# The first sixteen rows of the modulation matrix's five pieces on ScalarE's queue

## The chip, the cores and the metric

The kernel runs on one core of one Trainium2 chip. The core has TensorE (PE, with its weight loads shown apart as PEld), VectorE (DVE), ScalarE (ACT), GpSimd (POOL) and SyncE (SP, which here only issues transfers). The metric is the device time of one execution in microseconds, the median over several runs; lower is better. Before the change it is 325.9 us, median of three runs between 325.29 and 326.6 us.

## The reference, cut to what matters

The program is one transformer block with adaptive layer norm: a vector `c` is turned into six vectors of 640 numbers, which shift, scale and gate the two halves of the block.

```python
# x: 1 x 2048 x 640, c: 1 x 640, w_mod: 640 x 3840, all bf16
mod = (silu(c) @ w_mod).reshape(1, 6, 1, 640)
sa, ca, ga, sb, cb, gb = (mod[:, i] for i in range(6))
h = layernorm(x) * (1 + ca) + sa          # sa, ca: the first 1280 columns of w_mod
x = x + ga * attention(h)                 # 32 heads of 20, a window of 256 keys
h = layernorm(x) * (1 + cb) + sb
x = x + gb * ((sigmoid(h @ w_gate) * (h @ w_up)) @ w_down)
```

The change concerns only how the first 1280 columns of `w_mod` reach the core. They make `sa` and `ca`, without which no row of the first norm can be multiplied by `wq`, `wk` or `wv`.

## The kernel before, in words

The 2048 rows are worked on in eight chunks of 256 rows (two blocks of 128). A chunk goes through norm, transposition, the products with `wq`, `wk` and `wv`, windowed attention, the output product, the second norm and the gated feed-forward part. TensorE works almost without a pause from its first product to its last.

All instructions are first collected as operations with their reads and writes. A written-out list of numbers, `PLAN`, then sets the order in which operations go to the engines: an entry divided by five is the operation's number, the remainder its engine (0 PE, 1 ACT, 2 DVE, 3 POOL, 4 SP). Each engine takes its operations strictly in that order, and an operation waits by semaphores for what it reads. A transfer is one operation (`dma`, line 533); it is issued by SP, or by ACT when the code says so.

The start of the program runs like this.

- SP issues three transfers of `x`: 256 rows of the second chunk (320 KB), then the two 128-row blocks of the first chunk (160 KB each). Behind them come the five pieces of `w_mod` that this case is about, then `wq` and `wk` in halves, more rows of `x`, `wv` and the other columns of `w_mod`.
- ACT issues one small transfer, the vector `c` (1.2 KB, tile `c_row`), then loads its function table and computes the tanh for `silu(c)` (lines 606 to 609). DVE spreads the result over the tile `silubc`.
- A piece of `w_mod` holds 128 of its 640 rows, one to a partition, and 1280 columns: 128 rows of 2560 bytes, 320 KB. The five pieces land side by side in the space of `wd`, the later weight of the feed-forward part, and the profile calls them `wd`. In the code they are `wm_ap[0]`, and `load_bulk` at line 593 issues them, one transfer and one resource `Rm[0][kt]` for each `kt` from 0 to 4.
- DVE takes the statistics of the first rows of `x` as soon as they are there (lines 741 and 743, tile `st`), POOL computes the inverse root (lines 747 and 749), DVE normalises (line 762, `x<-x,st`), and TensorE transposes the result (`M<-ident,x`).
- Between the transpositions TensorE forms `silu(c) @ w_mod` in five steps of ten products (`fnA`, called at line 724, in the profile `S<-silubc,wd`), one step for each piece, and DVE copies the ten numbers per partition out (`mA`, line 726). Then DVE, ACT and POOL scale and shift the transposed rows (`hT<-hT,mA`, lines 822 and 823), and the product with `wq` begins.
- Products with a tile of zeros (`zeros`, line 621, in the profile `S<-E`) keep TensorE occupied before and between these steps. The first ten of them are followed by the transpositions.

Of the kernel before, what the change touches and what calls it, by code (L numbers as in the profile page):

```python
# [305 lines left out]
def c_pe(n):  # L306
# [4 lines left out]
    76, 139, 89, 63, 84, 202, 94, 3, 8, 243, 38, 175, 245, 72, 182, 186, 192, 197, 99, 53, 58, 13, 33, 18, 48, 104,  # L311
    109, 114, 357, 352, 124, 119, 129, 134, 747, 362, 378, 383, 337, 342, 392, 767, 347, 752, 762, 205, 210, 215,
    220, 225, 230, 1164, 368, 373, 772, 757, 387, 440, 235, 450, 250, 255, 260, 265, 405, 270, 395, 275, 778, 280,
    285, 290, 295, 456, 447, 412, 783, 792, 787, 795, 835, 805, 302, 401, 144, 482, 462, 472, 477, 433, 423, 466,
    600, 605, 801, 842, 815, 67, 417, 427, 585, 590, 811, 436, 822, 596, 611, 485, 490, 535, 540, 500, 615, 505,
    497, 550, 622, 512, 1172, 546, 1187, 1167, 555, 650, 561, 655, 565, 572, 1182, 661, 635, 515, 625, 640, 647,
    1192, 521, 1540, 1177, 1198, 1203, 23, 28, 525, 1208, 631, 715, 825, 532, 154, 1454, 149, 169, 720, 727, 665,
    685, 690, 697, 1546, 1217, 831, 1555, 700, 705, 730, 672, 575, 735, 712, 675, 1462, 1213, 1561, 1224, 682, 1457,
    1570, 581, 905, 890, 920, 910, 925, 895, 1553, 1568, 43, 1477, 917, 932, 1576, 1610, 1467, 164, 901, 742, 1583,
    875, 1472, 1482, 1228, 1616, 1623, 1243, 1488, 1493, 845, 880, 887, 860, 1498, 850, 865, 974, 871, 1625, 979,  # L320
    1631, 1246, 857, 969, 1585, 1045, 1072, 1597, 1592, 950, 955, 1052, 1602, 961, 1640, 935, 940, 947, 985, 1015,
    984, 1646, 990, 1020, 2650, 1055, 997, 1231, 1503, 1238, 1027, 1067, 1000, 2656, 1062, 1005, 1280, 159, 1285,
    1291, 1638, 1030, 2670, 1653, 1012, 1122, 1607, 1507, 1655, 1662, 1117, 1035, 1435, 1112, 2676, 1440, 1041,
    2690, 1667, 1325, 1340, 2663, 2668, 2696, 1672, 1345, 1352, 1250, 1255, 2559, 314, 1514, 334, 329, 1102, 1107,
    1677, 3114, 174, 1330, 1337, 1261, 2710, 2703, 1446, 1265, 1270, 1295, 1420, 1300, 1310, 1682, 1687, 2562, 2716,
    1307, 1276, 2730, 1089, 1425, 1690, 1695, 2736, 1720, 1315, 2567, 2572, 2750, 1374, 1076, 1321, 2756, 1379,
    1702, 1432, 2577, 2708, 2683, 2728, 2688, 2743, 2723, 2748, 1725, 1355, 1735, 1740, 1705, 1732, 2582, 1526,
    1747, 2587, 1405, 1767, 1772, 2770, 1710, 1717, 2768, 2763, 2593, 2598, 2613, 1384, 2603, 1360, 2776, 1531,
    1367, 1777, 1757, 1752, 1762, 1521, 1390, 1395, 1402, 1516, 1536, 1410, 2790, 3122, 1417, 1389, 2807, 3117,
    2370, 3127, 2796, 2802, 309, 2375, 2355, 1125, 2382, 2830, 1152, 2360, 2367, 2812, 1783, 2608, 2788, 2618, 2415,  # L330
    2624, 2783, 2420, 2430, 2435, 2525, 2836, 1132, 2479, 1788, 2828, 1792, 1797, 2848, 2843, 2426, 2442, 2484,
    2850, 2400, 2460, 2530, 2856, 2868, 2628, 2537, 2510, 2515, 2445, 2521, 2870, 2876, 2405, 1084, 1804, 2412,
    2642, 2632, 2888, 2638, 2465, 2385, 2471, 2646, 2495, 2390, 2450, 2397, 2890, 2457, 2500, 2910, 2970, 2975,
    2985, 2990, 2863, 2823, 2896, 2507, 2996, 3132, 3137, 2982, 3205, 2915, 2489, 2494, 3211, 1156, 2922, 2883,
    1135, 2925, 1147, 2908, 2903, 2930, 2540, 2545, 2937, 2817, 1844, 1142, 3142, 3225, 1834, 2551, 1821, 1806,
    1813, 3148, 3218, 1818, 2940, 3231, 3237, 3242, 3153, 3168, 3158, 4284, 3095, 2945, 1910, 3100, 1827, 1915,
    2955, 3106, 2951, 3247, 3860, 3866, 3163, 1920, 1925, 1935, 1839, 2960, 1930, 1940, 1945, 3252, 1950, 3858,
    3223, 3173, 1868, 3878, 2966, 1961, 1099, 3880, 1955, 1995, 3262, 3257, 1967, 4302, 1970, 2000, 2005, 1975,
    4307, 1872, 3039, 324, 1094, 319, 3179, 3886, 1852, 3034, 3000, 1980, 1985, 1990, 2021, 2010, 3265, 2015, 3005,
    3011, 2030, 3270, 2027, 3277, 2035, 2055, 3900, 2060, 2065, 2070, 3873, 3898, 3853, 4312, 1882, 1887, 1857,  # L340
    1849, 3906, 3015, 2040, 2075, 3020, 3080, 2045, 3085, 1892, 3893, 3913, 3918, 3026, 3091, 2050, 3920, 2081,
    3926, 3280, 3295, 3285, 3292, 2090, 2095, 2100, 2105, 2110, 2115, 2120, 3940, 3300, 2125, 2141, 3044, 2087,
    3933, 3938, 5484, 3946, 3307, 2130, 2135, 2147, 3327, 2150, 3192, 2175, 2155, 2160, 2165, 2180, 2170, 2201,
    3960, 3977, 3972, 3050, 2185, 4287, 3982, 3055, 2190, 2195, 3049, 2235, 2210, 2215, 3966, 3061, 3196, 2207,
    2220, 4000, 3310, 2240, 2245, 2250, 2255, 2225, 2230, 3315, 1863, 1898, 1903, 1878, 4292, 5492, 1907, 3987,
    4006, 2261, 3322, 4020, 3065, 3332, 2267, 4026, 2310, 4013, 4018, 3070, 2270, 2275, 3077, 3342, 3347, 5487,
    3337, 2330, 4040, 3201, 3181, 3953, 3998, 3958, 4297, 3352, 5507, 5502, 3358, 4038, 2280, 2290, 2335, 4046,
    3186, 2315, 4060, 2320, 5512, 3363, 3367, 3372, 2287, 2340, 3379, 2327, 4053, 4033, 4058, 3993, 4066, 4078,
    2347, 4110, 4170, 4115, 4121, 4073, 4365, 4371, 2295, 2300, 2307, 4185, 4190, 2354, 4175, 4197, 4375, 4318,
    3393, 4181, 3382, 4323, 4332, 4387, 4381, 4392, 5048, 4140, 4145, 4151, 3388, 5497, 4327, 4080, 4085, 4155,  # L350
    4160, 5000, 5028, 3401, 4095, 4100, 4092, 4125, 5006, 4167, 4107, 5023, 4250, 4255, 4261, 4130, 4235, 4265,
    4136, 5060, 4270, 4220, 5013, 4225, 4232, 3430, 4240, 3396, 5066, 4397, 3435, 3440, 4247, 5018, 4276, 5033,
    5043, 5053, 5078, 5088, 5090, 5073, 3405, 3410, 3415, 3420, 3425, 3445, 3450, 3465, 3470, 3490, 5619, 5096,
    5108, 3495, 5120, 3500, 3505, 4204, 5103, 5113, 4402, 4412, 4219, 3456, 3510, 3475, 5083, 3480, 5126, 5058,
    3485, 3462, 3525, 3530, 3535, 3550, 3516, 3522, 3540, 3555, 3560, 3565, 3570, 3545, 3576, 3582, 5118, 4339,
    4407, 4361, 5038, 4346, 5130, 5147, 3610, 3615, 3620, 3625, 3630, 3585, 4343, 3590, 5518, 5523, 3595, 3600,
    4353, 5532, 5136, 3605, 3636, 5160, 5166, 3645, 3650, 5142, 5527, 5188, 5198, 3655, 3660, 3665, 3696, 3670,
    3675, 3680, 5539, 3685, 3642, 5183, 3690, 5220, 4460, 3702, 5208, 5218, 5226, 5203, 5213, 5178, 3730, 3735,
    3705, 3710, 3715, 3720, 3725, 3756, 3740, 5250, 5256, 4415, 4420, 4427, 5561, 3745, 3750, 3762, 4358, 4430,
    4435, 4442, 4209, 4445, 4450, 5233, 4214, 5243, 4465, 4457, 4472, 4492, 4497, 5565, 5571, 4477, 4482, 4487,  # L360
    5325, 5330, 5337, 5385, 5390, 5396, 5310, 5238, 5248, 5193, 5268, 5278, 5263, 5273, 5315, 5173, 5152, 5157,
    5322, 5280, 5285, 5575, 5355, 4502, 4508, 4513, 5291, 5295, 5300, 5592, 5360, 5367, 5340, 5345, 5352, 5587,
    5597, 5307, 5581, 6205, 6211, 6228, 6233, 6248, 3785, 3765, 3790, 6238, 6253, 5370, 3825, 6263, 5375, 5381,
    6265, 4517, 6218, 3770, 6271, 3805, 6243, 6223, 3830, 3795, 6278, 6295, 6283, 6258, 5541, 6293, 4522, 6301,
    6313, 6323, 4529, 4536, 5602, 3835, 3775, 5612, 3782, 3810, 3815, 3802, 6325, 6331, 5607, 3822, 3842, 5420,
    5425, 5431, 5650, 5620, 5625, 5655, 5662, 5632, 5665, 6308, 5670, 6318, 6288, 6335, 4533, 5677, 4553, 4555,
    6352, 5635, 5640, 5647, 4546, 6347, 4541, 4580, 6341, 4585, 4590, 5556, 4595, 4600, 6413, 4560, 6365, 4565,
    4570, 4575, 4615, 4620, 4625, 4630, 5419, 5697, 6371, 5702, 5707, 5547, 5404, 4635, 4640, 6393, 4645, 6425,
    4606, 4650, 4655, 4660, 4675, 4666, 4700, 4705, 4710, 5682, 4680, 4685, 4715, 6431, 4690, 4695, 5687, 5692,
    5713, 5718, 6423, 6383, 6443, 6408, 4672, 3849, 4720, 4760, 6455, 6388, 6398, 5414, 5722, 4726, 4735, 4740,  # L370
    6461, 4745, 4750, 5727, 5734, 6357, 6378, 6403, 6418, 6362, 4755, 4612, 4786, 4765, 4770, 4775, 4780, 6685,
    6691, 4795, 4800, 6473, 4792, 4805, 4810, 4815, 4820, 4825, 4732, 4830, 4835, 4840, 4880, 4885, 4890, 6438,
# [66 lines left out]
MW = 64  # L439
# [887 lines left out]
```

## Time and profile before

| | |
|---|---|
| median of three runs | 325.9 us (325.29 to 326.6) |
| the profiled execution's own time | 324.32 us |
| its span, first to last instruction | 322.6 us |
| PE busy | 316.8 us, 98% of the span |
| DVE, ACT, POOL busy | 62%, 67%, 60% |
| the chain that ended last | PE 89%, POOL 4%, ACT 3%, DVE 2%, DMA 1% |
| first product with `wq` | starts at 12.05 us |

Times in the profile count from the first instruction of the profiled execution. Its span is 1.7 us shorter than its own time, and its own time is 1.6 us below the median of the runs; what the change does is worked out inside the span and added to the median. In a row of a timeline the first number is the start and the second the length; a bracket at the end tells how long the engine stood idle before it and what ended that. In the chain of waits each row is a piece of the path that ended last, again start and length.

### The profile page before, as it was taken

The page shows a single profiled execution, that of the slowest core. Times are in us where ns is not written, and L with a number is a line of the kernel's source. Part 1 is how long each engine was busy: PE and PEld are TensorE (multiplying, and loading weights), DVE is VectorE, ACT ScalarE, POOL GpSimd, SP SyncE. Part 2 cuts the span into 40 slices and gives each one's busy share as a digit, 9 for nine tenths or more (in the row PEclk, how much of TensorE's full clock was granted, in tenths as well). Part 3 has the DMA queues.
Part 4 walks back from the last instruction along what each step waited for, and adds up shares of the span by engine and source line. Part 5 has one row for each costly group of instructions (what it writes and reads, how often), then busy time and mean ns, then how long its engine had stood idle before and what let it go on. Part 6 is the DMA issues. An engine that isn't in the chain of part 4 may idle for free.

```text
span 322.6 us, 11139 instructions
## 1 busy us (share of the span) xinstructions
PE 316.8 (98%) x4766; PEld 230.9 (72%) x4766; DVE 199.9 (62%) x424; ACT 214.6 (67%) x220; POOL 193.9 (60%) x334
## 2 busy tenths in 40 slices
PE   6999999999999999999999999999999999999997
PEld 2666656577776677766787667876788777877885
DVE  6796999677585545685557454676438453485422
ACT  1489999997798787859785858684768557200320
POOL 4338679788788596969393839585672836601000
PEclk9999999999999999999999999999999999999999
DMA  7999799999912343308250211420400021012111
GB/s 231 374 332 199 198 258 206 184 273 317 210 40 41 103 92 48 62 3 130 55 114 4 35 35 48 102 43 2 122 6 4 2 43 43 2 41 43 41 43 42
DMA packets 64619, 33.61 MB, mean 104 GB/s; under 512 B 49082, under 2 KB 63034, under 8 KB 64570
## 3 DMA queue, kind: packets, MB, share of 16 engines
q1 hardware_dynamic: 63744, 31.92, 42.3%
q10 hardware_dynamic: 826, 0.98, 0.9%
q8 instruction: 37, 0.61, 0.8%
q14 instruction: 12, 0.10, 0.1%
HBM read 18.35 MB, written 2.62 MB: 65 GB/s over the span
## 4 chain that ended last, share of the span: by engine, by line
PE 89%; POOL 4%; ACT 3%; DVE 2%; DMA 1%; issue 1%; SPq 0%; ACTq 0%; DVEq 0%; POOLq 0%
PE M L634 74%; PE S L635 8%; PE M L635 7%; POOL E L947 3%; ACT E L981 2%; DMA x<-in_A_x_dram 1%; DVE x L762 1%; DVE st L741 1%; POOL st L749 1%; POOL st L747 0%; ACT QT L664 0%; DVE hT L823 0%; DVE st L743 0%; ACT hT L777 0%; SPq L533 0%
## 5 line engine op out<-in xcount | busy, mean ns | idle before, releaser
L947 POOL TENSOR_SCALAR_AFFINE_SELECT E<-E 128x256 bf16<-128x256 bf16 (+2 forms) x234 | 149.3, 667 | 52.2 <-ACT E L981 34.5
L981 ACT ACTIVATE E<-S 128x2048 bf16<-128x2048 f32 x80 | 150.2, 1878 | 42.3 <-PE S L635 41.6
L634 PE MATMUL M<-h2T,wu 128*128 128x256 bf16 x480 | 66.4, 273 | 0.0
L634 PE MATMUL M<-h2T,wg 128*128 128x256 bf16 x480 | 65.8, 273 | 0.0
L1225 DVE SCALAR_TENSOR_TENSOR hh<-sig,M 128x512 bf16<-128x512 f32 x48 | 32.4, 681 | 43.8 <-ACT sig L1223 31.6
L634 PE MATMUL M<-wd,hh 128*128 128x320 bf16 (+2 forms) x396 | 56.4, 295 | 0.0
L634 PEld LDWEIGHTS M<-h2T,wu 128*128 128x128 bf16 x480 | 45.7, 98 | 8.1 <-issue 1.6
L634 PEld LDWEIGHTS M<-h2T,wg 128*128 128x128 bf16 x480 | 45.5, 98 | 8.3 <-issue 1.5
L634 PEld LDWEIGHTS M<-wd,hh 128*128 128x128 bf16 x396 | 37.0, 98 | 14.9 <-issue 1.4
L1223 ACT ACTIVATE sig<-M 128x512 f32<-128x512 f32 x48 | 28.4, 596 | 26.1 <-PE M L634 25.0
L635 PE MATMUL S<-QT,KT 20*64 20x64 bf16 (+5 forms) x1600 | 33.3, 231 | 0.5
L1112 DVE STREAM_TRANSPOSE T<-M 128x512 f32<-128x512 f32 x32 | 21.7, 698 | 12.2 <-PE S L635 10.0
L741 DVE BATCH_NORM_STATS2 st<-x 128x6 f32<-128x320 bf16 x64 | 28.3, 477 | 1.1 <-DMA x<-in_A_x_dram 0.8
L635 PEld LDWEIGHTS S<-QT,KT 20*64 20x64 bf16 (+1 forms) x1600 | 15.2, 99 | 18.4 <-ACT E L981 9.8
L634 PE MATMUL M<-wk,hT 128*128 128x320 bf16 x160 | 28.2, 300 | 0.0
L634 PE MATMUL M<-wv,hT 128*128 128x320 bf16 x160 | 28.0, 300 | 0.0
L634 PE MATMUL M<-wo,oT 128*128 128x320 bf16 x160 | 26.5, 300 | 0.0
L634 PE MATMUL M<-wq,hT 128*128 128x320 bf16 x160 | 26.0, 300 | 0.2 <-DVE hT L823 0.2
L1244 DVE TENSOR_TENSOR x<-M,x 128x320 bf16<-128x320 f32 (+2 forms) x33 | 15.4, 478 | 15.1 <-PE M L634 14.5
L1179 DVE TENSOR_TENSOR x<-M,x 128x320 bf16<-128x320 f32 x32 | 15.3, 487 | 13.6 <-PE M L634 13.0
L747 POOL TENSOR_SCALAR st<-st 128x2 f32<-128x2 f32 (+1 forms) x17 | 4.0, 233 | 32.7 <-DVE st L743 31.7
L635 PEld LDWEIGHTS M<-E,V 128*32 128x32 bf16 x960 | 19.9, 97 | 4.5 <-issue 2.2
(81 smaller groups left out, 298.9 us busy)
## 6 DMA issues: line engine op xcount, KB each, us to landing
x<-in_A_x_dram SPq DMA_DIRECT2D x11, 320.0 KB, 3.6
wd<-in_w_mod_dram SPq DMA_DIRECT2D x6, 320.0 KB, 5.0
wd<-in_B_w_down_dram SPq DMA_DIRECT2D x4, 480.0 KB, 5.3
out_dram<-x SPq DMA_DIRECT2D x5, 320.0 KB, 2.6
wg<-in_B_w_gate_dram SPq DMA_DIRECT2D x2, 576.0 KB, 6.9
wu<-in_B_w_up_dram SPq DMA_DIRECT2D x2, 576.0 KB, 6.2
wu<-in_w_mod_dram SPq DMA_DIRECT2D x1, 960.0 KB, 10.5
wq<-in_A_wqkv_dram SPq DMA_DIRECT2D x2, 400.0 KB, 6.7
```

The lines of the kernel that those rows point to most:

```text
L634: return e.matmul(o, l, r, start=st, stop=sp, skip_group_check=True)
L635: return e.matmul(o, l, r, start=st, stop=sp, tile_position=tp, skip_group_check=True)
L741: A("dve", lambda e, g, bi=bi, j=j: e.bn_stats(v(bi * 12 + j * 6, 6), src[bi].ap[:, j * 320:(j + 1) * 320]), 0.48, reads=[src[bi].r()], wr ...
L747: A("pool", lambda e, g, lo=lo, w=w: e.tensor_scalar(v(28 + lo, w), var()[:, lo:lo + w], EPS, None, op0=ALU.add), 0.2, reads=[st.r(("m", b ...
L749: A("pool", lambda e, g, lo=lo, w=w: e.tensor_tensor(v(30 + lo, w), v(28 + lo, w), mhalf[:, 0:w], op=ALU.pow), 0.71, reads=[st.r(("v", lo) ...
L947: return lambda e, eng: e.affine_select(dst(), src(), pattern=pattern, compare_op=ALU.is_ge, fill=0.0, base=base, channel_multiplier=mul)
L981: A("act", lambda e, eng: e.activation(dst(), src(Sp.ap), ACT.Exp, scale=SM_SCALE), 1.876, reads=[Sp.r()], writes=[E.r()], prio=3, tag=f"e ...
L1112: A("dve", lambda e, g, h=h: e.transpose(T1.ap[:, 512 * h:512 * h + 512], X[h].ap), 0.694, reads=[X[h].r()], writes=[T1.r(h)], prio=3.5, t ...
L1179: A("dve", lambda e, g, ps=ps, bi=bi, half=half: e.tensor_tensor(x1[bi].ap[:, half * 320:half * 320 + 320], ps.ap[:, 0:320], x1[bi].ap[:, ...
L1223: A("act", lambda e, g, pg=pg, sg=sg: e.activation(sg.ap[:], pg.ap[:], ACT.Tanh, scale=0.5), c_act(512), reads=[pg.r()], writes=[sg.r()], ...
L1225: A("dve", lambda e, g, pu=pu, sg=sg, f0=f0: e.scalar_tensor_tensor(out=hh.ap[:, f0:f0 + 2, :], in0=sg.ap[:].rearrange("p (a b) -> p a b", ...
L1244: A("dve", lambda e, g, ps=ps, bi=bi, c0=c0, n=n: e.tensor_tensor(x1[bi].ap[:, c0:c0 + n], ps.ap[:, 0:n], x1[bi].ap[:, c0:c0 + n], op=ALU. ...
```

## The change

The five pieces on SP's queue lose their first sixteen rows each: they now carry 112 rows, partitions 16 to 127. A new transfer on ACT's queue brings the sixteen rows of all five pieces at once: sixteen partitions, five rows of 2560 bytes in each. It has a resource of its own, `R_top`, and every one of the five steps of `silu(c) @ w_mod` now reads it too.

```diff
-    load_bulk(wm_ap[0], wm_src[:, :, 0:1280], Rm[0], 1.26, 0.2, "wm0")
+    R_top = R("wmtop")
+    dma(lambda: wm_ap[0][0:16, 0:5, :], lambda: wm_src[0:16, 0:5, 0:1280], 0.30, writes=[R_top], prio=0.2, tag="wmt", eng="act")
+    for kt in range(NDT):
+        p0 = 16 if kt < 5 else 0
+        dma(lambda kt=kt, p0=p0: wm_ap[0][p0:, kt:kt + 1, :], lambda kt=kt, p0=p0: wm_src[p0:, kt:kt + 1, 0:1280], 1.26,
+            writes=[Rm[0][kt]], prio=0.2 + 0.01 * kt, tag="wm0")
...
-        oA.append(A("pe", fnA, MW / 2400.0 * 10, reads=[Rm[0][kt], R_silubc], writes=[psA.r()], prio=0, lat=0.2, tag="modA", extra=wprev))
+        oA.append(A("pe", fnA, MW / 2400.0 * 10, reads=[Rm[0][kt], R_top, R_silubc], writes=[psA.r()], prio=0, lat=0.2, tag="modA", extra=wprev))
...
 PLAN = [
-    76, 139, 89, 63, 84, 202, 94, 3, 8, 243, 38, 175, 245, 72, 182, 186, 192, 197, 99, 53, 58, 13, 33, 18, 48, 104,
+    76, 91, 144, 89, 63, 84, 207, 99, 3, 8, 248, 38, 180, 250, 72, 187, 191, 197, 202, 104, 53, 58, 13, 33, 18, 48,
```

`NDT` is 5, so `p0` is always 16. The new operation is number 18, so all later numbers in `PLAN` grow by five; entry 91 puts it on ACT, second in the list. Apart from it no instruction changes its place on any engine.

The start of ACT's queue before, where `c_row` is the vector `c`:

```order
L291 UNCONDITIONAL_BRANCH [waits barrier_Pool_Activation_PE_DVE_SP_release]
L533 DMA c_row<-in_c_dram 5x128
L606 ACT_TABLE_LOAD
L606 ACTIVATE cth<-c_col 128x5 [waits sem_dve]
L664 ACTIVATE hT<-M 128x128 [waits sem_pe]
```

The same place in the changed kernel, whose lines from here on stand five lower in the file:

```order
L291 UNCONDITIONAL_BRANCH [waits barrier_Pool_Activation_PE_DVE_SP_release]
L533 DMA c_row<-in_c_dram 5x128
L533 DMA wd<-in_w_mod_dram 16x5x1280
L611 ACT_TABLE_LOAD
L611 ACTIVATE cth<-c_col 128x5 [waits sem_dve]
L669 ACTIVATE hT<-M 128x128 [waits sem_pe]
```

The new transfer stands behind `c` and ahead of the load of ScalarE's function table, so the table and the tanh that `silu(c)` needs are issued one transfer later.

The start of SP's queue before, with the three transfers of `x` and the five pieces:

```order
L291 UNCONDITIONAL_BRANCH [waits barrier_Pool_Activation_PE_DVE_SP_release]
L533 DMA x<-in_A_x_dram 128x2x640
L533 DMA x<-in_A_x_dram 128x640 x2
L533 DMA wd<-in_w_mod_dram 128x1280 x5
L533 DMA wq<-in_A_wqkv_dram 128x5x320 x2
L533 DMA wk<-in_A_wqkv_dram 128x5x320 x2
```

And in the changed kernel:

```order
L291 UNCONDITIONAL_BRANCH [waits barrier_Pool_Activation_PE_DVE_SP_release]
L533 DMA x<-in_A_x_dram 128x2x640
L533 DMA x<-in_A_x_dram 128x640 x2
L533 DMA wd<-in_w_mod_dram 112x1280 x5
L533 DMA wq<-in_A_wqkv_dram 128x5x320 x2
L533 DMA wk<-in_A_wqkv_dram 128x5x320 x2
```

Only the size of the five pieces differs; their number and their place behind `x` do not.

218 rows, old and new, of the table PLAN are left out of this document.

## The prediction

> **What bounds the kernel now.** I read the profile's page first, then the chain of waits over the first 16 us, because the change touches nothing later. The page:
>
> ```profile
> span 322.6 us, 11139 instructions
> PE 316.8 (98%) x4766; PEld 230.9 (72%) x4766; DVE 199.9 (62%) x424; ACT 214.6 (67%) x220; POOL 193.9 (60%) x334
> PE 89%; POOL 4%; ACT 3%; DVE 2%; DMA 1%; issue 1%; SPq 0%; ACTq 0%; DVEq 0%; POOLq 0%
> ```
>
> TensorE is busy all through, and only 1% of the chain that ended last is a transfer. That one is at the start (the chain of waits, start and length of each piece):
>
> ```profile
> 1.30 3.08 DMA x<-in_A_x_dram
> ...
> 4.41 1.28 DVE st L741 x3
> ...
> 6.20 0.59 POOL st L749
> 6.82 0.45 DVE x L762
> ...
> 8.84 0.41 DVE x L762
> ...
> 9.64 0.72 POOL st L749
> 10.39 0.81 DVE x L762 x2
> 11.19 0.09 DVE mA L726
> ...
> 11.38 0.55 DVE hT L823 x2
> ...
> 12.05 4.00 PE M L634 x31
> ```
>
> The path begins with the second transfer of x, in at 1.30 + 3.08 = 4.38 us, and runs without slack through VectorE and GpSimd to the first product with wq at 12.05. No piece of w_mod (wd in the profile) is on it. They are not waited for elsewhere either. The pieces' transfers, as a group, and the weight loads of the first and the fifth step that use them:
>
> ```profile
> L533 SPq DMA_DIRECT2D wd<-in_w_mod_dram x5: 432/432/432, 2.3 to 4.2; - x5
> ...
> DMA to landing us min/median/max: 4.5/5.2/5.9
> ```
>
> ```profile
> 7.77 0.39 PEld L634 LDWEIGHTS S<-silubc,wd 128*128 128x128 bf16 x10
> ...
> 10.38 0.55 PEld L634 LDWEIGHTS S<-silubc,wd 128*128 128x128 bf16 x10
> ```
>
> Issue plus landing gives 2.3 + 4.5 = 6.8 us for the first piece and 4.2 + 5.9 = 10.1 for the fifth, steps of 0.82 us. They are used at 7.77 and 10.38, so 1.0 and 0.3 us lie in between, and neither row has a bracket for a wait. TensorE comes late to them for its own reasons: it waits for x, as the transpositions ahead show.
>
> ```profile
> 2.72 4.44 PE L621 MATMUL S<-E 128*128 128x512 bf16 x10
> 7.32 0.40 PE L634 MATMUL M<-ident,x 128*128 128x128 bf16 x4 [0.16 <-DVE x L762]
> ...
> 8.12 0.59 PE L621 MATMUL S<-E 128*128 128x512 bf16 x2
> ...
> 10.60 0.45 PE L634 MATMUL S<-silubc,wd 128*128 128x64 bf16 x10
> 11.32 0.50 PE L634 MATMUL M<-ident,x 128*128 128x128 bf16 x6
> ```
>
> Even the end of the fifth step, 10.60 + 0.45 = 11.05, comes when VectorE is still at the x of the chain (10.39 + 0.81 = 11.20); the copy of mA behind it would gain nothing from an earlier step.
>
> **What the change gives.** Each piece on SP's queue shrinks from 320 to 280 KB, an eighth, so with 0.82 us a piece the fifth could land up to 5 x 0.82 / 8 = 0.5 us sooner. Nobody waits for it: the gain is **0**. SP still issues five transfers of 0.432 us; SP is not waited for. The bytes in all are the same, so wq and what follows it on the queue move neither way, except by what the queue loses or gains on the way.
>
> **What the change costs on ACT.** One more issue ahead of the function table (timeline, with SP's first issues above it):
>
> ```profile
> 0.79 1.43 SPq L533 DMA_DIRECT2D x<-in_A_x_dram  x3
> ...
> 0.79 0.57 ACTq L533 DMA_DIRECT2D c_row<-in_c_dram  x1
> 1.40 1.28 ACT L606 ACT_TABLE_LOAD   x1 [1.40 <-PEq L1312]
> 2.69 0.21 ACT L606 ACTIVATE cth<-c_col 128x5 f32<-128x5 bf16 x1
> ```
>
> ```profile
> 3.13 0.49 DVE L609 COPY silubc<-siluc 128x320 bf16<-128x320 bf16 x1
> 4.41 1.28 DVE L741 BATCH_NORM_STATS2 st<-x 128x6 f32<-128x320 bf16 x3 [0.78 <-DMA x<-in_A_x_dram]
> 5.60 0.19 DVE L743 BATCH_NORM_AGGREGATE st<-st 128x2 f32<-128x12 f32 x1
> 5.90 0.89 DVE L741 BATCH_NORM_STATS2 st<-x 128x6 f32<-128x320 bf16 x2
> ```
>
> An issue is 0.43 (SP) to 0.57 us (this row). Table, tanh and the copy to silubc come about 0.5 us later, the copy ends at 3.62 + 0.5 = 4.1, and VectorE then still waits for x until 4.38. The wait of 0.78 us covers it. Without that cover, or with an issue longer than 0.78 us, VectorE's statistics would start later by the excess. I take **0**.
>
> **What the change costs x.** This is the term that counts. The new transfer is issued at about 1.40 on ACT and can move from about 2.4 us: the first transfer of x is issued at 0.79 and the rows of the rates below show the engines half idle up to 2.5. Before, w_mod's first bytes stood behind all of x on one queue. Now 16 x 5 x 2560 bytes = 200 KB of it are on a second queue while x is under way, on the same DMA engines. The rates, over five stretches (length, busy time of each engine, clock, DMA share, GB/s):
>
> ```profile
> 1.90:2.50 0.60, 0.18 (x2) 0.12 (x3) 0.04 (x1) 0.60 (x1) 0.60 (x5) 1.00 0.62 53
> 2.50:4.00 1.50, 1.50 (x4) 0.56 (x5) 0.78 (x3) 0.39 (x2) 0.97 (x11) 1.00 0.96 351
> 4.00:5.20 1.20, 1.20 (x4) 0.45 (x3) 0.80 (x2) 0.00 (x0) 0.00 (x0) 1.00 0.96 166
> 5.20:6.20 1.00, 1.00 (x4) 0.37 (x3) 0.89 (x4) 0.00 (x0) 0.23 (x2) 1.00 1.01 378
> 6.20:10.00 3.80, 3.57 (x48) 2.01 (x47) 3.74 (x12) 0.28 (x1) 1.98 (x5) 1.00 1.04 386
> ```
>
> From 2.5 us on the engines are full (share 0.96), so whatever the new transfer moves, x loses. The third transfer of x also shows what happens where x gives way to w_mod:
>
> ```profile
> L533 SPq DMA_DIRECT2D x<-in_A_x_dram x1: 424/424/424, 1.8 to 1.8; - x1
> ...
> DMA to landing us min/median/max: 4.1/4.1/4.1
> ```
>
> It lands at 1.8 + 4.1 = 5.9. From x at 4.38 to the first piece at 6.75 (6.8 above) 480 KB arrive in 2.37 us, where 0.82 us for each 320 KB would make 1.23: 1.1 us are lost, and the row 4.00:5.20 shows where, at 166 GB/s with busy engines. That is the stretch in which w_mod is read for the first time. Whether that reading is the cause the trace does not tell.
>
> The bounds of the delay to x's second transfer, with 204,800 bytes:
> - below: **0**, if the engines serve SP's queue first, or if the new rows fit into the idle 38% of 1.90:2.50 (its 53 GB/s and share of 0.62 make that little).
> - at full rate: 204,800 / 386 GB/s = **0.53 us**.
> - at the rate of the stretch with w_mod's first rows: 204,800 / 166 = **1.23 us**.
> - above: stall and slow rate one after the other, 1.1 + 1.23 = **2.3 us**.
>
> I take **1.2 us**: the new transfer is w_mod's first read, so that row is the nearest. A gain is all but excluded, since x's second transfer cannot land sooner by a transfer that joins it; the only give is the 0.11 us before the statistics of the third transfer (5.60 + 0.19 to 5.90), and only if that transfer came sooner.
>
> From 4.38 the delay goes through one to one: statistics at 5.6 instead of 4.41, wq at about 13.25. The third transfer would have to be in by 5.90 + 1.2 = 7.1, the fifth piece by 10.38 + 1.2 = 11.6; both have more room than before. So has wq, issued behind the pieces. Past 12.05 the chain has no transfer in it that matters (DMA 1% in all, 3.1 us of x here), so nothing takes the delay back.
>
> **Sum.** 0 (pieces) + 0 (ACT) + 1.2 (x) = +1.2 us. On the profiled execution 324.32 + 1.2 = 325.5, a span near 323.8; on the median **325.9 + 1.2 = 327.1 us**, 0.37% more, which is inside what a measurement of this kernel tells from no change (about 0.5%, 1.63 us).
>
> **The rivals.**
> *Bandwidth alone.* The new rows move at the full rate and x loses 0.53 us: 326.4. For it: 378 to 386 GB/s as soon as the slow stretch is over. Against it: that stretch.
> *Hidden.* x keeps its place, or the new rows slip in unseen: 325.9. This is also the case in which the change does nothing that it says, because the pieces were never late. For it: x is issued 0.6 us before. Against it: the full engines from 2.5.
> *Clearly slower: the sixteen rows hold the engines.* All of them go to the first 16 of 128 partitions, an eighth of the memory's rows, while a full piece goes to all. If stall (1.1) comes on top of the bytes at full (0.53) to slow rate (1.23), x is 1.6 to 2.3 us late, 2.0 in the middle: 327.9. It decides from a delay of 1.63 on, that is x's second transfer after 6.0 us. For it: the engines stay busy in the slow stretch, so a slow packet blocks those behind it. Against it: no row here shows a transfer into few partitions with many bytes.
> [...]
> *The clock.* The ten zero products are about 0.43 us apart (4.44 us for ten), the pair at 8.12 0.2 us apart (0.59 less 0.38 of one), so TensorE doubles its pace around 7 us. The idle time ahead of the transpositions grows from 0.16 to 1.4 us. If the slow pace came back or stayed, the chain's 4.00 us of products from 12.05 would cost up to as much again: 327.1 + 1 to 4, say 329. Against it: the pace is up before the pause, and the pause is short beside the 4.4 us that it took.
> *Faster* needs a wait for w_mod that the trace does not have, or a queue without the stall of 1.1 us; of the latter only 0.11 us can reach the path: 325.8.
>
> **How the numbers follow.** Forecast (327.1) 0.36, bandwidth alone 0.27, hidden 0.12, sixteen rows hold the engines 0.18, clock 0.05, faster 0.02. The range leaves out the clock, the top of the slower case and the lower half of the hidden one: **325.7 to 328.0 us**. Slower by over 0.5% (above 327.53) are the clock, nearly all of the slower case and about a tenth of the forecast's weight: 0.26. Faster by over 0.5% (below 324.27): 0.02. Within 0.5%: 0.72.
>
> **What would show it.** In the changed profile the first statistics on VectorE start near 5.6 instead of 4.41, still ended by a transfer of x, and every later row up to wq (13.25) is as much later; the silubc copy ends near 4.1; the steps with w_mod show no wait for a transfer. The ACT transfer lands before 5.6. Right by the wrong way would be a later start whose bracket names silubc or ACT. Wrong would be statistics at 4.4 (then hidden), at 4.9 (bandwidth alone) or past 6.0 (slower), products after 7 us at half the pace (clock), or a step that waits for w_mod or wq.

## The result, and the profile after

The change made the kernel slower: 329.22 us median of six runs (328.57 to 329.35) against 325.88 us (324.52 to 326.8, six runs), a ratio of 1.0105 with a 95% interval of 1.0084 to 1.0126. The forecast was 327.1, within 325.7 to 328.0.

The page of the changed kernel. All line numbers from 594 on are five higher than before.

```profile
span 327.5 us, 11141 instructions
PE 318.1 (97%) x4766; PEld 232.0 (71%) x4766; DVE 199.6 (61%) x424; ACT 214.6 (66%) x220; POOL 194.4 (59%) x334
PE 88%; POOL 3%; DMA 3%; ACT 3%; DVE 1%; issue 1%; SPq 0%; ACTq 0%; DVEq 0%; POOLq 0%
```

The share of transfers in the chain that ended last went from 1% to 3%. Its start, from the chain of waits over the first 20 us (start, length):

```profile
1.30 5.31 DMA x<-in_A_x_dram
...
6.64 1.28 DVE st L746 x3
...
9.05 0.46 DVE x L767
...
10.52 0.83 PE S L626 x2
11.35 0.53 PE S L639 x10
...
14.71 0.18 DVE mA L731
...
15.66 4.41 PE M L639 x34
```

The second transfer of x takes 5.31 us instead of 3.08, so the statistics start at 6.64 instead of 4.41: **2.23 us**. From there to the first product with wq it was 7.64 us before (4.41 to 12.05) and is 9.02 now (6.64 to 15.66): another **1.38 us**, and the chain now runs through TensorE's zero products (L626) and the steps with w_mod (`S L639`), which were not on it before. The timelines of TensorE and VectorE at this place:

```profile
3.22 4.19 PE L626 MATMUL S<-E 128*128 128x512 bf16 x10
9.56 0.40 PE L639 MATMUL M<-ident,x 128*128 128x128 bf16 x4 [2.14 <-DVE x L767]
...
10.35 1.00 PE L626 MATMUL S<-E 128*128 128x512 bf16 x2
11.14 0.74 PE L639 MATMUL S<-silubc,wd 128*128 128x64 bf16 x10
```

```profile
3.73 0.49 DVE L614 COPY silubc<-siluc 128x320 bf16<-128x320 bf16 x1
6.64 1.28 DVE L746 BATCH_NORM_STATS2 st<-x 128x6 f32<-128x320 bf16 x3 [2.42 <-DMA x<-in_A_x_dram]
```

TensorE stands idle for 2.14 us ahead of the transpositions. Soon behind that the pair of zero products takes 1.00 us instead of 0.59, and the second step's ten products with w_mod 0.74 instead of 0.46, which were these before:

```profile
8.55 0.46 PE L634 MATMUL S<-silubc,wd 128*128 128x64 bf16 x10
```

The granted clock, by stretches (length, busy time of each engine, clock, DMA share, GB/s):

```profile
3.58:7.00 3.42, 3.42 (x9) 1.21 (x8) 0.96 (x3) 0.00 (x0) 0.00 (x0) 1.00 1.10 203
7.00:10.40 3.40, 1.26 (x19) 0.73 (x18) 3.12 (x11) 0.14 (x1) 1.04 (x3) 1.00 1.05 300
10.40:13.80 3.40, 3.40 (x38) 2.31 (x34) 2.64 (x8) 0.53 (x2) 1.53 (x3) 0.50 1.11 326
13.80:17.00 3.20, 2.98 (x41) 1.98 (x39) 2.18 (x10) 2.00 (x5) 0.84 (x2) 1.00 1.12 368
```

For 3.4 us TensorE runs at half the clock, right behind a stretch in which it was busy for 1.26 us of 3.40. The column shows this fall, but not the slow pace at the start of the program: it reads 1.00 in 3.58:7.00 too, where the ten zero products take 0.42 us each, about twice the later time (the pair at 14.51 takes 0.60 us and a single one 0.38, so 0.22 from one to the next). Whether the pace has come up at all must be read from the products.

A third loss comes later, at a wait for a transposing transfer. The same products before, and now:

```profile
33.71 0.40 PE L635 MATMUL S<-QT,KT 20*128 20x256 bf16 x8
```

```profile
38.54 0.40 PE L640 MATMUL S<-QT,KT 20*128 20x256 bf16 x8 [1.15 <-DMA QT<-stg]
```

The products of TensorE are 3.61 us late up to there and 4.83 us from there, and the span ends 4.95 us later (322.56 to 327.51). That is more than the medians differ, 3.34 us: the first profile of the kernel before, 324.32 us, was one of its quick executions. The experiments had to explain three things: why x is late, whether the half clock is the price of the pause, and whether the wait for QT belongs to the change.

### The profile page after: what moved, and what is told of

Its sections match the earlier page's. It is cut to its first block, busy times and chain, and to the rows that moved or that the text cites. A ratio compares the mean times of both kernels' runs of the same rounds, so it can differ in the third digit from the quotient of the medians.

```text
span 327.5 us, 11141 instructions
## 1 busy us (share of the span) xinstructions
PE 318.1 (97%) x4766; PEld 232.0 (71%) x4766; DVE 199.6 (61%) x424; ACT 214.6 (66%) x220; POOL 194.4 (59%) x334
## 4 chain that ended last, share of the span: by engine, by line
PE 88%; POOL 3%; DMA 3%; ACT 3%; DVE 1%; issue 1%; SPq 0%; ACTq 0%; DVEq 0%; POOLq 0%
PE M L639 72%; PE S L640 8%; PE M L640 7%; POOL E L952 3%; ACT E L986 2%; DMA x<-in_A_x_dram 2%; DMA QT<-stg 1%; PE S L626 1%; PE S L639 1%; POOL st L754 0%; DVE st L746 0%; DVE x L767 0%; ACT QT L669 0%; DVE hT L828 0%; ACT hT L782 0%
## 5 line engine op out<-in xcount | busy, mean ns | idle before, releaser
L639 PE MATMUL M<-h2T,wu 128*128 128x256 bf16 x480 | 66.4, 273 | 0.0
L639 PE MATMUL M<-h2T,wg 128*128 128x256 bf16 x480 | 65.8, 273 | 0.0
L639 PE MATMUL M<-wd,hh 128*128 128x320 bf16 (+2 forms) x396 | 56.4, 295 | 0.0
L639 PEld LDWEIGHTS M<-h2T,wu 128*128 128x128 bf16 x480 | 45.7, 98 | 8.2 <-issue 1.6
L639 PEld LDWEIGHTS M<-h2T,wg 128*128 128x128 bf16 x480 | 45.6, 98 | 8.2 <-issue 1.5
L639 PEld LDWEIGHTS M<-wd,hh 128*128 128x128 bf16 x396 | 37.0, 98 | 14.9 <-issue 1.4
L639 PE MATMUL M<-wk,hT 128*128 128x320 bf16 x160 | 28.2, 300 | 0.0
L639 PE MATMUL M<-wv,hT 128*128 128x320 bf16 x160 | 28.0, 300 | 0.0
L639 PE MATMUL M<-wo,oT 128*128 128x320 bf16 x160 | 26.5, 300 | 0.0
L639 PE MATMUL M<-wq,hT 128*128 128x320 bf16 x160 | 26.0, 300 | 0.2 <-DVE hT L828 0.2
```

Source lines behind the costliest of these rows:

```text
L639: return e.matmul(o, l, r, start=st, stop=sp, skip_group_check=True)
```

## The experiments

Theories at the start: **narrow**, the sixteen partitions of the ACT transfer make it hold the transfer engines while x is on them; against it **share**, any 200 KB beside x would cost as much. For the second loss: **clock** against slower pieces of w_mod.

### The same bytes over all partitions

```diff
-    dma(lambda: wm_ap[0][0:16, 0:5, :], lambda: wm_src[0:16, 0:5, 0:1280], ..., eng="act")
+    dma(lambda: wm_ap[0][:, 0:1, 0:800], lambda: wm_src[:, 0:1, 0:800], ..., eng="act")
...
-        p0 = 16 if kt < 5 else 0
+        c0 = 800 if kt < 1 else 0     # the pieces on SP: all rows, columns c0 to 1279
```

> The ACT transfer carries as many bytes (204,800) at the same place, but over all 128 partitions: 800 columns of the first piece, whose other 480 columns stay on SP's queue; pieces two to five are whole again. Theory 'narrow': it is the 16 partitions that make the transfer hold the engines, so here x pays its bytes alone, 0.5 to 0.8 us: statistics at 4.9 to 5.2, wq at 12.6 to 12.9, time up to 0.8 us above before (326.4 to 326.7), pieces in steps of 0.82 us. Rival 'share': any 200 KB of w_mod on a second queue beside x cost x 2.2 us: statistics at 6.6, time near 329.

VectorE's timeline, and the pieces on SP's queue as a group:

```profile
4.57 1.28 DVE L746 BATCH_NORM_STATS2 st<-x 128x6 f32<-128x320 bf16 x3 [0.55 <-DMA x<-in_A_x_dram]
```

```profile
L533 SPq DMA_DIRECT2D wd<-in_w_mod_dram x5: 432/432/441, 2.3 to 4.2; - x5
...
DMA to landing us min/median/max: 3.5/4.2/5.1
```

x is 0.16 us late, less than even "narrow" expected (0.5 to 0.8), wq starts at 12.27 and the time is 325.6 us against 325.81, ratio 1.0000 (0.9985 to 1.0016). Even the fifth piece lands sooner than before, 4.2 + 5.1 = 9.3 instead of 10.1, and nothing that can be told comes of it. "Share" falls: the second queue and the bytes cost next to nothing here (0.16 us), the shape does (2.23 us).

### The ACT transfer later

```diff
+PLAN.remove(91)
+PLAN.insert(PLAN.index(191) + 1, 91)     # 191: the tanh
```

> The changed kernel with the ACT transfer issued behind the tanh (about 2.9 instead of 1.4 us), so that most of x is in before it moves. Both theories of the delay: statistics at 4.4 to 4.8. It tells what is left of the loss when x is spared: 'narrow' lets the transfer and the 112-row pieces slow each other, fifth piece at 11.5 to 12.5, the fifth step of silu(c) @ w_mod waits for it, wq at 12.5 to 13.5 and 0.5 to 1.4 us above before; 'share' has the fifth piece at about 10.0 and the time of before (325.9).

```profile
4.37 1.28 DVE L748 BATCH_NORM_STATS2 st<-x 128x6 f32<-128x320 bf16 x3 [0.74 <-DMA x<-in_A_x_dram]
...
7.69 0.89 DVE L748 BATCH_NORM_STATS2 st<-x 128x6 f32<-128x320 bf16 x2 [1.94 <-DMA x<-in_A_x_dram]
```

The second transfer of x is on time, but the third is caught: its statistics start at 7.69 instead of 5.90. wq starts at 14.81, later than both theories said: the expectation counted only the pieces, not the third transfer of x, and TensorE was at the slow pace (its pair of zero products takes 1.04 us behind a pause of 1.78). The time is 328.45 us, ratio 1.0114 (1.0083 to 1.0146): no better than the change.

### The sixteen rows on SP's queue, behind x

```diff
-    dma(lambda: wm_ap[0][0:16, 0:5, :], ..., eng="act")
+    dma(lambda: wm_ap[0][0:16, 0:5, :], ..., eng="sp")
+PLAN.remove(91)
+PLAN.insert(PLAN.index(99), 94)          # ahead of the five pieces
```

> The changed kernel with the sixteen-row transfer issued by SP, behind x and ahead of the five 112-row pieces, so that x has the engines for itself. Theory 'narrow': statistics at 4.4, the sixteen-row transfer takes about 2 us by itself and the 112-row pieces land in steps of 0.95 us, so the fifth is in at about 12 and the first product with wq starts at 13.3 to 14.3. Rival, only the meeting with x is slow: 0.5 us for the sixteen rows, steps of 0.72 us, fifth at about 9.9, wq at 12.05.

The six transfers of w_mod as a group, and what waited for them:

```profile
L535 SPq DMA_DIRECT2D wd<-in_w_mod_dram x6: 424/427/432, 2.3 to 4.6; - x6
...
  PEld S L641: 2.3, 5
  PE S L641: 0.7, 3
...
DMA to landing us min/median/max: 4.5/5.8/7.0
```

With x spared (statistics at 4.32), the loss moves to w_mod. The sixteen rows land at 2.3 + 4.5 = 6.8, when before a whole piece was in; the last 112-row piece at 4.6 + 7.0 = 11.6 instead of 10.1. That is (11.6 - 6.8) / 5 = 0.96 us for a piece of 280 KB, where 320 KB took 0.82. Now the steps wait for their pieces, and wq starts at 13.16, just ahead of the range expected (one execution, 326.53 us, beside 326.81 for the kernel before, so the time itself shows no loss). The sixteen rows cost 1.2 us here, not 2: the third transfer of x is in at 5.6, they are in at 6.8. But the 112-row pieces are slow in themselves too; "only the meeting with x" falls.

### Fewer bytes

```diff
-    dma(lambda: wm_ap[0][0:16, 0:5, :], ...
+    dma(lambda: wm_ap[0][0:16, 0:2, :], ...
-        p0 = 16 if kt < 5 else 0
+        p0 = 16 if kt < 2 else 0
```

> The ACT transfer carries the sixteen rows of the first two pieces only (80 KB), pieces three to five are whole again. Theory 'narrow' with a delay that grows with the bytes: two fifths of 2.24, statistics at about 5.3, wq at 12.9 to 13.3; the two 112-row pieces in steps of 0.95, the whole ones in steps of 0.82. Rival, a fixed price for the meeting: statistics at 6.4 to 6.7 as in the changed kernel.

Statistics at 5.23: 0.82 us late for 2/5 of the bytes, where 2/5 of 2.23 is 0.89. The delay goes with the bytes. wq starts at 14.27, a microsecond later than expected: from the statistics to wq it takes 9.04 us, as in the changed kernel, and TensorE is at the slow pace again (one execution, 327.66 us). This is not a fall of the clock like that of the changed kernel. There the first products behind the pause are still quick; here they are slow at once and the ten zero products ahead of the pause were slow too (4.47 us), while the clock column, which shows the fall there, stays at 1.00. So the pace had not come up yet:

```profile
8.15 0.61 PE L639 MATMUL M<-ident,x 128*128 128x128 bf16 x4 [0.95 <-DVE x L767]
```

### The same rows into unused space, near and far

The five pieces are whole again, and the ACT transfer copies 204,800 bytes of w_mod to space that nothing reads yet: this adds bytes and leaves no work out.

```diff
+    dma(lambda: Eall[0:16, 2:6, :].rearrange("p s c -> p (s c)")[:, 0:6400]...,     # near
+    dma(lambda: Eall[0:128:8, 2:6, :].rearrange("p s c -> p (s c)")[:, 0:6400]...,  # far
         lambda: wm_src[0:16, 0:5, 0:1280], ..., eng="act")
```

> The five pieces are whole (128 rows) on SP's queue as before; the ACT transfer of 200 KB still reads the same sixteen rows of each piece at the same place, but writes them to space that is not used yet, partitions 0 to 15. It is a copy that nothing reads, 200 KB more than before moves. Theory 'narrow' (sixteen neighbouring partitions take the bytes slowly): x as late as in the changed kernel, statistics at 6.2 to 6.8, but the whole pieces then follow in steps of 0.82 us. Rival, that the 112-row pieces make x late: statistics at 4.4 to 5.0.

> The same copy into unused space, to every eighth partition (0, 8, ... 120) instead of 0 to 15: same source, queue, bytes and number of rows. Theory 'narrow by place' (the neighbouring partitions share a way in): half as much delay or less, statistics at 4.6 to 5.4. Rival 'narrow by number' (sixteen partitions anywhere, or 12.8 KB into one partition, are slow): statistics at 6.2 to 6.8 as with partitions 0 to 15.

Near: statistics at 6.57, so the sixteen-row transfer alone makes x late, without any 112-row piece; the whole pieces follow in steps of 0.82 us (7.8 to 11.1), as expected. Far: statistics at 4.44, but the comparison is not clean. ScalarE needed 0.68 us to issue it instead of 0.34, so it moved later (from 3.2 to 3.6 us one packet of it moves, 41 with near), and it then caught the third transfer of x (statistics of that at 6.89 instead of 5.90). By these times, number or place stays open; the next section has a measure that decides it.

### Number or place

The same copy, to 32, 64 and 128 partitions; the bytes are always 204,800. If place counts, the two copies to 64 partitions differ; if the number alone does, they are alike.

```diff
+    dma(lambda: Eall[0:32, ...][:, 0:3200],  lambda: wm_src[0:32, 0, 0:3200], ..., eng="act")
+    dma(lambda: Eall[0:64, ...][:, 0:1600],  lambda: wm_src[0:64, 0, 0:1600], ..., eng="act")
+    dma(lambda: Eall[32:96, ...][:, 0:1600], lambda: wm_src[32:96, 0, 0:1600], ..., eng="act")
+    dma(lambda: Eall[0:128, ...][:, 0:800],  lambda: wm_src[0:128, 0, 0:800], ..., eng="act")
```

> The same copy to partitions 0 to 31, 6400 bytes in each. [...] Rival 'number': about twice the delay of 64 partitions, half of that of 16: statistics at 5.3 to 5.7 here, but 4.7 to 5.0 with 64.

> As spare_near (whole pieces on SP's queue, a copy of 204,800 bytes that nothing reads on ACT's), but to partitions 0 to 63 with 3200 bytes in each. [...] Rival 'number': the delay falls with the number of partitions (2.2 at 16, 0.2 at 128), 64 give 0.3 to 0.6: statistics at 4.7 to 5.0.

> The same copy to 64 partitions that lie elsewhere, 32 to 95. [...] Rival 'number': the same as with 0 to 63, within 0.15 us.

> The same copy to all 128 partitions, 1600 bytes in each: the measure for the other three. Both theories: x late by its bytes alone at most, 0.1 to 0.5 us, statistics at 4.5 to 4.9; the pieces of w_mod behind it 0.5 us later than before at most.

The stretch from 3.8 to 4.8 us, in which the copy and x share the engines (columns as above, the last is GB/s), with partitions 0 to 15:

```profile
3.80:4.80 1.00, 1.00 (x3) 0.30 (x2) 0.19 (x1) 0.00 (x0) 0.00 (x0) 1.00 1.03 113
```

With 0 to 31:

```profile
3.80:4.80 1.00, 1.00 (x3) 0.30 (x2) 0.18 (x1) 0.00 (x0) 0.00 (x0) 1.00 1.00 193
```

With 0 to 63:

```profile
3.80:4.80 1.00, 1.00 (x3) 0.30 (x2) 0.39 (x1) 0.00 (x0) 0.00 (x0) 1.00 1.01 243
```

With 32 to 95:

```profile
3.80:4.80 1.00, 1.00 (x4) 0.41 (x3) 0.97 (x4) 0.00 (x0) 0.00 (x0) 1.00 0.98 319
```

With all 128:

```profile
3.80:4.80 1.00, 1.00 (x3) 0.30 (x2) 0.47 (x2) 0.00 (x0) 0.00 (x0) 1.00 1.14 402
```

| partitions | statistics start | late by | third transfer of x in | time, one execution | issue on ACT |
|---|---|---|---|---|---|
| 0 to 15 | 6.57 | 2.16 | 7.0 | 327.99 | 0.34 |
| 0 to 31 | 5.73 | 1.32 | 6.1 | 327.02 | 0.34 |
| 0 to 63 | 4.95 | 0.54 | 6.1 | 326.29 | 0.53 |
| 32 to 95 | 4.38 | 0 | 5.7 | 324.29 | 0.60 |
| 128 | 4.63 | 0.22 | 5.4 | 325.66 | 0.38 |

In all five the transfer engines are busy all the time (shares of 0.98 to 1.14), and the rate climbs from 113 to 402 GB/s. (The kernel before moves 216 GB/s in this stretch, with no copy at all: it has the slow stretch of w_mod's first read there. So the rates rank the five copies, and do not say what a copy costs.) The delay of the statistics mixes two things, how slow the copy is and how much of x's second transfer it meets. The issues differ by up to 0.26 us, and from 3.2 to 3.6 us 20 packets of the copy move with 0 to 31, 5 with 0 to 63 and none with 32 to 95. That can be why 0 to 31 looks 0.8 us worse than 0 to 63 here, although the third transfer of x lands at 6.1 with both.

A measure without that is the time that the copy's own packets take on the 16 engines. The rows of ACT's queue, which carries nothing else of size, from 3 to 6 us (packets, MB, share of the 16 engines' time), with 0 to 15 and with every eighth partition:

```profile
q10 hardware_dynamic: 96, 0.20, 34.9%
```

```profile
q10 hardware_dynamic: 96, 0.20, 25.0%
```

With 0 to 63, and with 32 to 95:

```profile
q10 hardware_dynamic: 80, 0.20, 22.7%
```

```profile
q10 hardware_dynamic: 80, 0.20, 18.1%
```

Each pair has the same bytes, the same number of partitions and the same number of packets, and its two edits differ by place alone: place counts, and number alone falls. The share is 20.9% with 0 to 31, close to the 22.7% with 0 to 63, and 18.2% with all 128, close to the 18.1% with 32 to 95. The second of each pair also starts later, but an early start is not what raises the share: the 200 KB over all partitions of the first experiment start earlier than 0 to 63 (12 packets from 3.2 to 3.6 us) and have 18.2% too. Why 0 to 31 and 0 to 63 still differ a little is open; they also differ in what each partition takes (6400 and 3200 bytes).

### The clock: a shorter pause, and a longer one

The changed kernel with eight zero products more, and the kernel before with four fewer:

```diff
-HEAT = (5, 1, 1, 1, 1, 1, 1)
+HEAT = (13, 1, 1, 1, 1, 1, 1)     # in the changed kernel
+HEAT = (1, 1, 1, 1, 1, 1, 1)      # in the kernel before
```

> The changed kernel with 8 more zero products in the first block, so that TensorE is busy from 3.2 to about 9.0 us. Theory 'clock': the granted clock fell to half from 10.4 to 13.8 us because TensorE stood idle for 2.1 us behind the zero products; with the pause filled it stays up, x is as late as in the changed kernel (statistics at 6.64), and the first product with wq comes at about 14.3 instead of 15.66, 1.3 us or so off the time of the changed kernel: near 327.9. Rival: the 1.4 us between 9.56 and 15.66 come from something else (late pieces of w_mod, slower engines); then wq stays near 15.7 and the time near 329.2.

> The kernel before with 4 zero products fewer in the first block: TensorE is idle from about 5.3 to 7.3 us while x and w_mod are on time. Theory 'clock': statistics at 4.41 as before, clock at half until about 10.4, wq at 13.2 to 13.4 instead of 12.05, 1.2 us slower than before (327.1). Rival, the clock does not matter in this stretch: wq within 0.2 us of 12.05 and no difference in time.

TensorE in the changed kernel with more zero products:

```profile
2.73 5.63 PE L626 MATMUL S<-E 128*128 128x512 bf16 x18
9.32 0.40 PE L639 MATMUL M<-ident,x 128*128 128x128 bf16 x4 [0.96 <-DVE x L767]
...
10.12 0.60 PE L626 MATMUL S<-E 128*128 128x512 bf16 x2
```

And in the kernel before with fewer:

```profile
2.72 2.77 PE L621 MATMUL S<-E 128*128 128x512 bf16 x6
7.21 0.61 PE L634 MATMUL M<-ident,x 128*128 128x128 bf16 x4 [1.71 <-DVE x L762]
...
8.69 1.04 PE L621 MATMUL S<-E 128*128 128x512 bf16 x2
```

With the pause cut to 0.96 us the pair is back at 0.60 us, and statistics to wq take 7.65 us (6.40 to 14.05): the whole 1.38 us is gone with x still late. Its median is 328.03 us, 1.2 us below the changed kernel's from the earlier comparison, ratio to the kernel before 1.0091 (1.0066 to 1.0116). So the pause is what the 1.38 us hang on, and slower pieces are not needed for it. In the other, with x on time, the same stretch grows to 9.21 us (4.29 to 13.50), and the time is 326.82 against 325.81, ratio 1.0047 (1.0024 to 1.0070). But this is a neighbouring case, not the same one: its six zero products are slow (2.77 us) and so are the first products behind the pause (0.61), with 1.00 in the clock column throughout. There the pace came up late; it did not fall.

### The wait for QT in the kernel before

The kernel before, unchanged, twice more, and once with the transfer of wo that stands between the transposing transfers put ahead of them:

```diff
+PLAN.remove(164)
+PLAN.insert(PLAN.index(169) + 1, 164)    # wo ahead of the first transposing transfer
```

> The kernel before once more, to see an execution other than the one profiled at first (324.32). Theory 'chance': the wait of 1.15 us for a transposing transfer (QT<-stg) at 38.5 us of the changed kernel is not the change's doing; it is in most executions of the kernel before too, and an execution near 325.9 shows it, at 33.7 us, with everything up to there as in the first profile. Rival 'knock-on': the late start of the changed kernel causes it; then no execution of the kernel before shows it, and one near 325.9 loses its time elsewhere.

> As before_again: a further execution of the kernel before. By 'chance' an execution above 325.5 has a wait of about 1 us for QT<-stg near 33.7 us and one below 325 has none; by 'knock-on' neither has it.

> The kernel before with SP's first transfer of wo issued ahead of the transposing transfer of hT instead of behind it, at about 14.3 instead of 25.05 us, so that SP's issue of 1.26 us no longer stands between the transposes. Theory 'chance': QT<-stg is issued about a microsecond sooner, the wait goes, and the time settles near 324.4 instead of 325.9, 0.4% less. Rival: the wait comes from the transfers themselves or from more bytes ahead of hT; no difference, or up to 1.2 us slower.

The first took 324.95 us and has no such wait. The second took 326.75 us, and its waits between 30 and 40 us have the row

```profile
PE S L635 <- DMA QT<-stg: 1.4, 1, 1.4
```

Its wq starts at 13.01 instead of 12.05. TensorE's pace came up later (the single zero product ahead of the pair takes 0.63 us instead of 0.38), but the path goes elsewhere: four of the five steps wait for their piece of w_mod, and the chain of waits from 6 to 14 us begins with the last piece, in at 4.16 + 7.35 = 11.51 instead of 10.1.

```profile
7.69 0.63 PE L621 MATMUL S<-E 128*128 128x512 bf16 x1
...
8.58 0.60 PE L621 MATMUL S<-E 128*128 128x512 bf16 x2
```

```profile
4.16 7.35 DMA wd<-in_w_mod_dram
...
11.56 0.48 PE S L634 x10
```

So the kernel before has the wait for QT now and then, without the change, and "knock-on" in its strict form falls: the wait is no mark of the change. The runs above agree. It is absent with the copy to partitions 0 to 15, whose x is as late as in the changed kernel, and there with 128 partitions (1.07 us), whose x is not. A weaker form stays open: a wait of 0.4 to 1.4 us is there in 9 of the 12 profiled executions with an added transfer of w_mod, and in 1 of the 5 in which w_mod came as before. With wo ahead, ten runs had a median of 324.78 us (324.49 to 325.61) against 325.64 (324.17 to 326.15), but the ratio, 0.999, has an interval of 0.9972 to 1.0008: no difference that can be told.

## Why the prediction was wrong

Two steps failed. The term for the delay of x, 1.2 us, measured 2.23; and the clock, which cost 1.38 us more, was set beside that delay as a rival instead of behind it as its consequence.

- **Right, but only for the execution that was read: the gain of 0.** The pieces were not waited for there, and landing them 0.8 us sooner, with the bytes spread over all partitions, bought nothing that can be told. The slack of 0.3 us was thinner than one profile shows: in another execution of the kernel before one step waited 0.2 us for its piece, and in the third profile the last piece was on the path. That the gain is 0 on the median was in part luck.
- **Right: ACT's issue at no cost.** It took 0.34 us; the copy to silubc ends at 3.73 + 0.49 = 4.22, where 4.1 was expected, and VectorE's bracket names x.
- **Mis-sized: the delay to x.** The term was 1.2 us with bounds of 0 and 2.3; it measured 2.23. I took the slow stretch of w_mod's first read as the nearest row, and that was the wrong kin: as many bytes of w_mod, read at the same time, cost 0.16 us when they go to 128 partitions. What the term needed was a row for a transfer into few partitions, and the trace had none. The rival "the sixteen rows hold the engines" was the true case, at 0.18, with 2.0 us and its place right, though the stall of 1.1 us that I added up for it did not show with those 128.
- **Which partitions: what the runs show.** In the stretch that the copy and x share, 113 GB/s move with 0 to 15, 193 with 0 to 31, 243 with 0 to 63, 319 with 32 to 95 and 402 with all 128. 0 to 31 and 0 to 63 are close in the engines' time for the copy (20.9 and 22.7%), 32 to 95 and all 128 too (18.1 and 18.2%), though 0 to 31 made x's second transfer 0.8 us later than 0 to 63. By what way the place acts no run shows.
- **Wrong: the clock as a rival of its own.** I gave it 0.05 and said that the pace "is up before the pause, and the pause is short". It fell nevertheless, behind a stretch in which the pause of 2.14 us left TensorE busy for only 1.26 of 3.40 us; with the pause cut to 0.96 us it did not. The step that failed is setting it beside the delay of x; it follows from it. The late x is what makes the pause. The slower case alone would have been 2.0 + 1.4 = 3.4 us, 329.3, on the measured median. Its price, 1 to 4 us, was taken from products with wq that were not touched; what it cost was 1.38 us, on products between the transpositions.
- **Wrong, without effect here: the 112-row pieces.** I made them an eighth quicker (0.72 us). They are slower than whole ones, 0.96 us. In the changed kernel TensorE comes later than they do; with x spared they become the wait. Why they are slower no run tells.
- **The base.** The sum was made against an execution of 324.32 us, 1.6 us below the median, which I carried as a constant. In part it is the wait for QT (1.4 us) and late pieces of w_mod, which come and go in the kernel before: the third profile has both. That fits the spans differing by 4.95 us and the medians by 3.34; how often each occurs was not measured.

## What to carry to other kernels

Moving a small slice of a transfer to a second queue did not take it off the first queue's path here when it landed in a few neighbouring partitions: 200 KB into sixteen of them held up x by 2.2 us, and as many bytes over all 128 by 0.2 us. Cut off along the columns, 200 KB left the time as it was (ratio 1.0000); cut off along the partitions, they cost 3.3 us. If a transfer must be cut, try the columns first. When something early becomes late, ask at once what the waiting engine does in the longer pause, here whether TensorE's clock outlasts it: that loss came on top, 1.38 us.

## What was not expected of the hardware

- The slow transfer slowed x without an idle engine to be seen: the DMA share is 1.03 in the stretch with 113 GB/s and 1.14 in that with 402.
- 112 rows of 2560 bytes took 0.96 us, behind the sixteen rows on SP's queue, where 128 rows took 0.82 in the kernel before.
- Behind a pause of 2.14 us the clock fell to half for 3.4 us, and the fall came 0.84 us after the pause had ended (9.56 to 10.40). In the 3.40 us before the fall TensorE was not idle all the time: 1.26 us of work did not keep the clock. It fell in the same way with the copy to partitions 0 to 15, behind 1.11 us of work in 3.40. With a pause of 0.96 us behind a longer run of zero products it stayed, and behind a pause of 1.44 us, with the copy to 0 to 31, the products were quick too:

```profile
8.64 0.40 PE L641 MATMUL M<-ident,x 128*128 128x128 bf16 x4 [1.44 <-DVE x L769]
```

With 0.95 us, in the run with two pieces, they were slow because the pace had not come up. So the length of the pause alone did not decide here; whether there is a limit of length at all, somewhere between 1.44 and 2.14 us, is not shown.
